# Branch C of the first input gradient chunks by three products, in a convolution stem with group norm and gelu, forward and backward

## The chip, the cores and the metric

The kernel runs on one core of a Trainium2 chip. The metric is device time in microseconds (us) of one execution; lower is better. The engines are TensorE (PE, with weight loads as PEld), VectorE (DVE), ScalarE (ACT), GpSimd (POOL) and the transfer queue that SyncE (SP) issues. Each engine works through its own instructions in a fixed order and waits on semaphores of the others.

## The reference

A strided convolution (stride 2, 31 taps, 256 channels in and out), a normalization over time for each batch and channel, and gelu. All of it is computed together with the gradients for a given `grad_out`:

```python
B, T, D, K = 2, 16000, 256, 31
s = 2
L = (T - K) // s + 1                       # 7985
h = sum(einsum('blc,cd->bld', x[:, i:i + s * L:s, :], w[i]) for i in range(K))
mu = einsum('bld->bd', h)[:, None, :] / L
var = einsum('bld->bd', (h - mu) ** 2)[:, None, :] / L
h = (h - mu) / sqrt(var + 1e-5)
h = h * gn_gamma[None, None, :] + gn_beta[None, None, :]
out = gelu(h)                              # tanh form
out, vjp = jax.vjp(f, x, w, gn_gamma, gn_beta)
grads = vjp(grad_out)                      # of x, w, gn_gamma, gn_beta
```

Inputs and outputs are bf16.

## The kernel before

*Fewer products.* A polynomial product of two halves can be formed with three smaller products instead of four. The kernel nests this over three binary digits of the tap index. The outer two digits are called branch (`br`) and leaf (`lf`); each takes a value of A, B_ or C_, where B_ works on differences or sums of the two halves. So every chunk of time has nine (branch, leaf) products, and a leaf can be cut a third time.

*Three parts.* The forward convolution runs for 2 batches x 4 chunks x 3 branches (stages `F0a` to `F1z`, about 0 to 412 us). The input gradient (`input_grad`, stages `G0a` to `G1z`, about 412 to 822 us) runs over batch `b`, chunk `c`, branch in the order B_, A, C_, and two halves `pr`. The weight gradient (`weight_grad`, stages `Wa` to `Wz`) is the rest. The gelu of batch 0 runs beside the forward pass of batch 1, the gelu of batch 1 (`gelu_batch(1, ...)`, eight units) beside the first input gradient chunks: its gradients are needed when the gradient of batch 1 begins.

*One unit of the input gradient.* There are two forms. `plain` uses the three-way cut for leaf B_ alone (4 matmuls in `g_three_b`, 8 in `g_three_ac`), copies the negated sum to a second accumulator, and then adds leaf A and leaf C_ with 16 matmuls each (`g_leaf`): 44 matmuls. `split` cuts all three leaves: 12 matmuls each, 36 in all. For this, leaves A and C_ need differences of weights (`W2D`, made by `w2_sub`) and the sums that `outer()` makes, and a join (`VP`) of leaf B_ with branch B_'s result. The set `GV` names the chunks that take `split`: in the kernel before, all from chunk (0, 3) on.

*From accumulator to output.* There are four accumulator slots of two banks (`ring`). In each unit ScalarE writes a negated half or whole accumulator (lines 1396 and 868 to `ps`), and `keep` (line 868) copies an accumulator to SBUF as bf16. In `plain`, branches A and C_ are joined with branch B_ by a VectorE instruction that reads the accumulator (`g_join`, line 1411, rate 1); in `split`, a keep writes the output tile `HO` first, and the join reads SBUF. Two tiles `HO` take turns, and `g_store` writes each to memory.

*Around it.* `e_load`, `e_comp` and `e_spread` prepare the next chunk's gradient of `h`: the tiles `EG` and `ET`. `e_spread` copies the two-column overlap of neighbouring chunks (`cp`, line 1296, four GpSimd copies a chunk) and spreads the rest with ScalarE copies (line 1305). A gelu unit loads a half tile of `h`, makes `y` and its square on ScalarE (line 1155), their product with one fused VectorE instruction (line 1157), two sigmoids (lines 1159 and 1161), several VectorE products (line 1167) and sums (line 1180 on ScalarE, 1183 on VectorE). SBUF is one `arena`, divided by hand by byte offsets: tiles overlay each other over time.

*What sets the order.* `Plan.add` records each operation with the tiles it reads and writes. `Plan.order` gives every operation a due time from its successors and a lead from the table `lead`, keyed by stage, helper and caller, lists them on modelled engines, and `emit` issues them in the order of these starts. So the numbers of the table move instructions on all engines. `plan.hold` keeps an operation behind a given matmul; `XPAT` says at which unit of the forward pass each of the eight blocks of x sums (`x_pre`) may be issued.

Of the kernel before, what the change touches and what calls it, by code (L numbers as in the profile page):

```python
# [30 lines left out]
def act(n, extra=0.0):  # L31
    return 0.06 + n * 0.00097 + extra
# [6 lines left out]
class Plan:  # L39
# [3 lines left out]
    def __init__(self, tc):  # L43
# [11 lines left out]
            "F0 conv_stem_kernel wrapper": 109.4,  # L55
            "F0 f_evac last": -1.7,
            "F0 f_join f_evac": 2.6,
            "F0 f_join split": 3.7,
            "F0 f_mm f_three_ac": -0.5,
            "F0 f_mm f_three_b": 0.7,  # L60
            "F0 f_three_b split": -75.0,
            "F0 keep f_evac": 5.3,
            "F0 keep split": -9.5,
            "F0 load conv_stem_kernel": 43.4,
            "F0 load f_evac": 2.8,
            "F0 load put": 0.4,
            "F0 load x_pre": 4.0,
            "F0 load_gb conv_stem_kernel": -22.9,
            "F0 tt f_sums": -3.6,
            "F0 tt second": 5.1,  # L70
            "F0 tt third": -3.4,
            "F0 turn w2_part": 1.2,
            "F0 turn x_load": -6.2,
            "F0 w_sub w2_part": -1.6,
            "F0 x_pre conv_stem_kernel": -0.1,
            "F0 zero conv_stem_kernel": 30.6,
            "F0 zero f_evac": -6.0,
            "F0 zero w2_part": -47.0,
            "F0 zero x_load": -17.6,
            "F0a f_evac last": 8.9,  # L80
            "F0a f_join f_evac": -2.0,
            "F0a f_join split": -16.3,
            "F0a f_mm f_leaf": -12.0,
            "F0a f_mm f_three_b": -24.3,
            "F0a f_mm pe_turn": 7.0,
            "F0a f_three_b f_first": 6.4,
            "F0a f_three_b split": -2.1,
            "F0a keep f_first": -23.9,
            "F0a keep split": -2.3,
            "F0a load load_w": 15.6,  # L90
            "F0a load x_load": 13.2,
            "F0a put x_first": -3.4,
            "F0a tt f_sums": -2.8,
            "F0a tt second": -0.3,
            "F0a tt third": -2.7,
            "F0a turn x_load": -35.7,
            "F0a ve f_first": -3.4,
            "F0a w_sub f_first": -2.1,
            "F0a zero load_w": -15.4,
            "F1 f_evac last": 3.7,  # L100
            "F1 f_join f_evac": 10.3,
            "F1 f_mm f_leaf": 0.3,
            "F1 f_mm f_three_ac": -0.5,
# [1832 lines left out]
```

## Time and profile before

| | us |
|---|---|
| median of three timed runs | 1120.94 (1117.76 to 1122.73) |
| profiled execution, its own time | 1115.62 |
| its span | 1113.8 |
| PE, VectorE, ScalarE, GpSimd busy in the span | 1080.7, 997.6, 605.8, 37.4 |
| first real matmul | 17.86 |
| first matmul of the input gradient | 412.74 |
| mean bandwidth of the transfers | 235 GB/s |

The profile is one execution. Busy times are unions: the records of neighbouring instructions overlap a little. A matmul's record is longer than its share of PE's time, since matmuls overlap too; what one costs is read from how many fit into a full stretch. In the rows of instruction groups, the number behind the bar is the busy time, then follow the mean duration of one in ns and, behind the second bar, the idle time ahead of them and what ended it. In rows of waits the numbers are total, times and longest. In rows in order of time, the first two numbers are start and duration, and a bracket holds the wait ahead.

### The profile page before, as it was taken

The page shows a single profiled execution, that of the slowest core. Times are in us where ns is not written, and L with a number is a line of the kernel's source. Part 1 is how long each engine was busy: PE and PEld are TensorE (multiplying, and loading weights), DVE is VectorE, ACT ScalarE, POOL GpSimd, SP SyncE. Part 2 cuts the span into 40 slices and gives each one's busy share as a digit, 9 for nine tenths or more (in the row PEclk, how much of TensorE's full clock was granted, in tenths as well). Part 3 has the DMA queues.
Part 4 walks back from the last instruction along what each step waited for, and adds up shares of the span by engine and source line. Part 5 has one row for each costly group of instructions (what it writes and reads, how often), then busy time and mean ns, then how long its engine had stood idle before and what let it go on. Part 6 is the DMA issues. An engine that isn't in the chain of part 4 may idle for free. (4 is left out here: it accounts for less than half of the span.)

```text
span 1113.8 us, 19741 instructions
## 1 busy us (share of the span) xinstructions
PE 1080.7 (97%) x8094; PEld 795.8 (71%) x8132; DVE 997.6 (90%) x1039; ACT 605.8 (54%) x838; POOL 37.4 (3%) x67
## 2 busy tenths in 40 slices
PE   5999999999999999999999998999999999999998
PEld 4888899888888984444444443444468888888887
DVE  6995968789999996999899988889789999999996
ACT  1244444688788649797767566676643323332232
POOL 0000000000000010020200011000000000000000
PEclk9999999999999999999999999999999999999999
DMA  9369999995979699987675999988797655696974
GB/s 227 54 178 242 278 268 270 256 175 147 193 169 244 211 288 311 263 231 237 179 244 149 318 317 290 292 286 284 253 297 228 229 205 165 242 326 206 301 213 124
DMA packets 346894, 261.47 MB, mean 235 GB/s; under 512 B 187702, under 2 KB 315572, under 8 KB 340916
## 3 DMA queue, kind: packets, MB, share of 16 engines
q1 hardware_dynamic: 346612, 260.22, 82.4%
q8 instruction: 63, 1.03, 0.4%
q14 instruction: 27, 0.22, 0.1%
q0 software_dynamic: 192, 0.00, 0.0%
HBM read 120.00 MB, written 94.86 MB: 193 GB/s over the span
## 5 line engine op out<-in xcount | busy, mean ns | idle before, releaser
L814 PE MATMUL ps<-arena 128*128 128x256 bf16 (+3 forms) x3668 | 396.7, 271 | 17.0 <-DMA arena<-in_x_dram 7.7
L1369 PE MATMUL ps<-arena 128*128 128x512 bf16 (+1 forms) x1834 | 400.6, 377 | 8.9 <-ACT arena L868 4.2
L814 PEld LDWEIGHTS <-arena 128*128 128x128 bf16 x3668 | 359.0, 99 | 54.4 <-DMA arena<-in_x_dram 8.2
L1369 PEld LDWEIGHTS <-arena 128*128 128x128 bf16 x1872 | 183.6, 98 | 225.2 <-issue 11.7
L868 ACT ACTIVATE arena<-ps 128x1024 bf16<-128x1024 f32 (+1 forms) x187 | 190.0, 1022 | 240.5 <-PE ps L1659 118.5
L1659 PE MATMUL ps<-arena 128*128 128x256 bf16 x2592 | 284.0, 273 | 3.0 <-DVE arena L1613 2.3
L1659 PEld LDWEIGHTS <-arena 128*128 128x128 bf16 x2592 | 253.2, 98 | 34.0 <-DVE arena L1613 3.6
L782 DVE TENSOR_TENSOR arena<-arena 128x2064 bf16<-128x2064 bf16 (+5 forms) x132 | 164.1, 1266 | 26.6 <-PE ps L814 22.8
L1167 DVE TENSOR_TENSOR arena<-arena 128x2048 bf16<-128x2048 bf16 (+1 forms) x80 | 95.4, 1194 | 9.4 <-ACT arena L1159 4.4
L1332 DVE TENSOR_TENSOR arena<-arena 128x1032 bf16<-128x1032 bf16 (+7 forms) x111 | 86.0, 796 | 5.3 <-PE ps L1369 4.8
L1396 ACT ACTIVATE ps<-ps 128x512 f32<-128x512 f32 x108 | 62.8, 586 | 25.3 <-PE ps L1369 25.1
L1155 ACT ACTIVATE arena<-arena,stats 128x1024 bf16<-128x1024 bf16 (+1 forms) x64 | 74.5, 1207 | 1.3 <-DVE stats L1101 0.8
L1555 DVE TENSOR_TENSOR arena<-arena 128x1536 bf16<-128x1536 bf16 (+3 forms) x56 | 62.3, 1124 | 13.3 <-DMA d2d<-arena 12.2
L1622 DVE TENSOR_TENSOR arena<-arena 128x4096 bf16<-128x4096 bf16 x32 | 72.2, 2285 | 0.4 <-DMA arena<-in_x_dram 0.3
L844 ACT ACTIVATE ps<-ps 128x512 f32<-128x512 f32 x59 | 34.3, 582 | 70.2 <-PE ps L814 70.1
L1411 DVE TENSOR_TENSOR arena<-arena 128x1024 bf16<-128x1024 bf16 (+1 forms) x70 | 63.3, 914 | 9.4 <-ACT arena L868 9.0
L1731 ACT COPY ps<-ps 128x512 f32<-128x512 f32 x54 | 30.8, 571 | 64.7 <-PE ps L1659 64.7
L1718 DVE TENSOR_TENSOR arena<-arena 128x2048 bf16<-128x2048 bf16 x54 | 64.7, 1218 | 0.3 <-DMA arena<-d2d 0.3
L1613 DVE TENSOR_TENSOR arena<-arena 128x4096 bf16<-128x4096 bf16 (+1 forms) x32 | 62.1, 1952 | 0.1
L1665 DVE TENSOR_TENSOR arena<-arena 128x1024 bf16<-128x1024 bf16 x75 | 48.8, 684 | 7.8 <-ACT arena L868 7.7
L890 ACT ACTIVATE arena<-ps 128x512 bf16<-128x512 f32 (+1 forms) x64 | 36.7, 579 | 34.8 <-PE ps L814 34.5
L767 DVE TENSOR_TENSOR arena<-arena 128x2048 bf16<-128x2048 bf16 (+1 forms) x45 | 50.5, 1147 | 1.4 <-DMA vl<-arena 1.4
(72 smaller groups left out, 536.9 us busy)
## 6 DMA issues: line engine op xcount, KB each, us to landing
arena<-in_x_dram SPq DMA_DIRECT2D x28, 1024.0 KB, 9.6
arena<-d2d SPq DMA_DIRECT2D x16, 1216.0 KB, 7.4
out_dram<-arena SPq DMA_DIRECT2D x35, 512.0 KB, 4.1
d2d<-arena SPq DMA_DIRECT2D x30, 384.0 KB, 5.6
arena<-dnd SPq DMA_DIRECT2D x10, 960.0 KB, 6.2
arena<-vl SPq DMA_DIRECT2D x9, 1024.0 KB, 8.7
hd<-arena SPq DMA_DIRECT2D x8, 1024.0 KB, 6.8
arena<-in_x_dram SPq DMA_DIRECT2D x32, 256.0 KB, 4.9
```

The costliest lines, as they stand in the source:

```text
L782: lambda: nc.vector.tensor_tensor(out=o, in0=a, in1=b, op=ALU.add))
L814: yield nc.tensor.matmul(ps[:, dh, cs], lhsT=wt, rhs=mv, start=s0, stop=False, skip_group_check=True)
L868: lambda: nc.scalar.activation(out=out, in_=ps, func=ACT.Copy, scale=scale))
L1155: lambda o=o, func=func, i=h[:, dh], sc=sc, bi=bi: SC.activation(out=o, in_=i, func=func, bias=bi, scale=sc))
L1167: add("DVE", dve(8 * wd), [o], [a, b_], lambda: V.tensor_tensor(out=o, in0=a, in1=b_, op=op))
L1332: lambda: nc.vector.tensor_tensor(out=o, in0=a, in1=b, op=ALU.add))
L1369: yield nc.tensor.matmul(ps[:, e, 0:wide], lhsT=lt, rhs=mv, start=s0, stop=False, skip_group_check=True)
L1396: lambda: nc.scalar.activation(out=ps[:, 1], in_=ps[:, 0], func=ACT.Copy, scale=-1.0))
L1411: add("DVE", dve(o.free_size(), rate), [o], [a, b], lambda: nc.vector.tensor_tensor(out=o, in0=a, in1=b, op=op))
L1622: add("DVE", dve(4096), [o], [a, b], lambda: nc.vector.tensor_tensor(out=o, in0=a, in1=b, op=ALU.add))
L1659: yield nc.tensor.matmul(ps[:, s, c0:c1], lhsT=lt, rhs=mv, start=s0, stop=False, skip_group_check=True)
L1718: add("DVE", dve(2048), [d4], [d], lambda: nc.vector.tensor_tensor(out=d4, in0=fan(d[:, o0:o0 + 3 * s + 1:s, :], 1, (o1 - o0) * D), in1=fa ...
```

## The change

Seven edits stand in one diff.

1. `GV` now names branches, and branch C_ of chunks (0, 0), (0, 1) and (0, 2) takes the form `split`. Its two weight differences are made before the first chunk (`w2_outer(True)`), the other four at the old place. `W2D` is laid out anew, so that branch C_'s differences lie at 94208.
2. The gelu tiles `h` of batch 1, which lay there, move to `GREG + 12544` (139968 and 144064), over buffers of the forward pass (`U`, `RB`).
3. In `plain`, branches A and C_ are now kept in `HO` by ScalarE and joined in SBUF. After edit 1 this form is left to branch A.
4. The overlap copies of `e_spread` go from four on GpSimd to two on ScalarE, and its memsets and those of `e_comp` at chunk ends to VectorE.
5. The fused VectorE instruction of gelu (line 1157) becomes an addition of a constant and a product.
6. `leaf_d` of the weight gradient takes both batches in one instruction.
7. `XPAT` issues the eight blocks of x sums at other units, the first at (0, 0, A), and the whole table `lead` has other numbers.

```diff
-            "F0 conv_stem_kernel wrapper": 109.4,
-            "F0 f_evac last": -1.7,
+            "F0 conv_stem_kernel wrapper": 139.4,
+            "F0 f_evac last": -6.4,
...
-    W2D = {(MIR[br], lf): sb(o + 4096 * i, 2, 2, 512) for lf, o in ((B_, 73728), (C_, 94208), (A, 106496)) for i, br in enumerate(ORDER)}
+    W2D = {(MIR[br], B_): sb(73728 + 4096 * i, 2, 2, 512) for i, br in enumerate(ORDER)}
+    W2D.update({(MIR[br], lf): sb(94208 + 8192 * i + 4096 * j, 2, 2, 512) for i, br in enumerate((C_, B_, A))
+                for j, lf in enumerate((A, C_))})
...
-        add("DVE", dve(8 * wd, 1), [z], [y2, y],
-            lambda: V.scalar_tensor_tensor(out=z, in0=y2, scalar=1.0 / GELU_A, in1=y, op0=ALU.add, op1=ALU.mult))
+        add("DVE", dve(8 * wd, 4), [z], [y2],
+            lambda: V.tensor_scalar(out=z, in0=y2, scalar1=1.0 / GELU_A, scalar2=None, op0=ALU.add))
+        add("DVE", dve(8 * wd), [z], [z, y], lambda: V.tensor_tensor(out=z, in0=z, in1=y, op=ALU.mult))
...
-            zero(EG[:, :, 0, 0, 231:HM], 50)
-            zero(EG[:, :, 0, 1:4, 230:HM], 156)
-            zero(EG[:, 0, 1, :, 230:HM], 104)
-            zero(EG[:, 1, 1, :, 230:HM], 104)
+            v = EG.rearrange("p d e k f -> p d (e k) f")
+            zero(v[:, :, 0, 231:HM], 50, "DVE")
+            zero(v[:, :, 1:8, 230:HM], 364, "DVE")
...
-            def cp(o, i):
-                add("POOL", 0.3, [o], [i], lambda: nc.gpsimd.tensor_copy(out=o, in_=i))
-            for dh in range(2):
-                cp(et[:, dh, 0:3, :, 0:2], et[:, dh, 0:3, :, 256:258])
-            cp(et[:, :, 3, 0, 0:2], et[:, :, 3, 0, 256:258])
-            cp(et[:, :, 3, 1, 0:1], et[:, :, 3, 1, 256:257])
+            for o, i in ((ev[:, :, 0:7, 0:2], ev[:, :, 0:7, 256:258]), (ev[:, :, 7, 0:1], ev[:, :, 7, 256:257])):
+                add("ACT", act(o.free_size()), [o], [i], lambda o=o, i=i: nc.scalar.copy(out=o, in_=i))
...
-    GV = {(b, c) for b in range(NB) for c in range(NCK) if (b, c) >= (0, 3)}
+    EARLY = (C_,)
+    GV = {(b, c, br) for b in range(NB) for c in range(NCK) for br in ORDER if (b, c) >= (0, 3) or (br in EARLY and c in (0, 1, 2))}
...
+                elif True:
+                    keep(ho[:, :, j, :], ps[:])
+                    g_join(ho[:, :, j, :], ho[:, :, j, :], rb, ALU.subtract if (br == A) == (lf == A) else ALU.add, 2)
...
-                        (split if (b, c) in GV else plain)(b, c, pr, br, P * pr, sums)
+                        (split if (b, c, br) in GV else plain)(b, c, pr, br, P * pr, sums)
...
-                for b in range(NB):
-                    o_ = 2 if i3 == A else 0
-                    add("DVE", dve(2304), [DL[i3, b]], [D2[b]], lambda b=b, i3=i3, o_=o_: nc.vector.tensor_tensor(
-                        out=DL[i3, b], in0=D2[b][:, o_:o_ + 17:2, :], in1=D2[b][:, 1:18:2, :], op=ALU.subtract))
+                o_ = 2 if i3 == A else 0
+                w_two("leaf_d", [DL[i3, b] for b in range(NB)], [t[:, o_:o_ + 17:2, :] for t in D2], [t[:, 1:18:2, :] for t in D2], ALU.subtract, D2)
...
-          {"h": (94208, 98304), "y": (102400, 106496), "s": (110592, 114688), "y2": (GREG,), "z": (GREG + 4096,), "o": (), "g": (GREG + 8192,)})
-    XPAT = {u: i for i, u in enumerate([(0, c, br) for c in range(1, 4) for br in ORDER][:4 * len(PRE)])}
+          {"h": (GREG + 12544, GREG + 16640), "y": (102400, 106496), "s": (110592, 114688), "y2": (GREG,), "z": (GREG + 4096,), "o": (), "g": (GREG + 8192,)})
+    XPAT = {(0, 0, A): (0,), (0, 1, B_): (1, 2), (0, 1, C_): (3,), (0, 2, A): (4,), (0, 2, C_): (5,), (0, 3, B_): (6, 7)}
...
+    w2_outer(True)
     ge = gelu_batch(1, GT[1], *PACE[1])
...
-            w2_outer()
+            w2_outer(False)
```

Two places show what this does to the order. The first is ScalarE in chunk (0, 0), where branch C_ begins. Line 1396 (1403 after the change) is a half negation, line 868 (880) to `ps` a whole negation and to `arena` a keep, line 1305 (1312) a spread copy, 1155 (1167) gelu's `y` and square, 1159 and 1161 (1172 and 1174) its sigmoids, 1180 (1193) its sums. Before:

```order
L1396 ACTIVATE ps0_114<-ps0_114 128x512
L1305 COPY arena_110<-arena_110 128x3x256 x4
L1305 COPY arena_110<-arena_110 128x2x256
L868 ACTIVATE ps1_115<-ps0_114 128x1024
L1305 COPY arena_110<-arena_110 128x2x256
L1159 ACTIVATE arena_110<-arena_110 128x2048
L1161 ACTIVATE arena_110<-arena_110 128x2048
L1396 ACTIVATE ps2_116<-ps2_116 128x512
L1155 ACTIVATE arena_110<-arena_110,stats_101 128x1024 x2
L868 ACTIVATE ps3_117<-ps2_116 128x1024
L1180 ACTIVATE arena_110,esum1_108<-arena_110 128x1024
```

After, at the same place of the chunk:

```order
L1172 ACTIVATE arena_110<-arena_110 128x2048
L880 ACTIVATE arena_110<-ps3_117 128x2x512
L880 ACTIVATE arena_110<-ps0_114 128x1024
L1403 ACTIVATE ps2_116<-ps2_116 128x512
L1174 ACTIVATE arena_110<-arena_110 128x2048
L1403 ACTIVATE ps0_114<-ps0_114 128x512
L880 ACTIVATE arena_110<-ps1_115 128x2x512
L1403 ACTIVATE ps3_117<-ps3_117 128x512
L880 ACTIVATE arena_110<-ps2_116 128x2x512
L1312 COPY arena_110<-arena_110 128x3x256
L1403 ACTIVATE ps1_115<-ps1_115 128x512
L1312 COPY arena_110<-arena_110 128x2x256
```

Between two sigmoids of one gelu unit now stand two keeps and a half negation, and keeps of 2 x 512 to the output tile stand among the spread copies, where before two whole negations and gelu's own instructions stood.

The second place is the transfer queue of SP where the forward pass ends: `hd1_0` is `h` of batch 1, chunk 0 (half tiles of 2 x 1024 for gelu), `vl1`, `vl2` and `vl0` are the input gradient's weights of branches B_, C_ and A, the two transposes from `arena` turn the first chunk's gradient, and `dnd0` takes it. Before:

```order
L609 DMA arena_110<-hd1_0_64 128x2x1024
L609 DMA arena_110<-dyd0_0_68 128x4096
L609 DMA arena_110<-hd1_0_64 128x2x1024
L609 DMA arena_110<-vl1_58 128x4x1024 x3
L609 DMA arena_110<-vl2_59 128x4x1024 x3
L614 DMA_TRANSPOSE arena_110<-arena_110 128x16x128 x2
L614 DMA_TRANSPOSE arena_110<-in_grad_out_dram 128x8x256
L609 DMA hd1_3_67<-arena_110 128x4096
```

After:

```order
L619 DMA arena_110<-vl1_58 128x4x1024 x2
L619 DMA arena_110<-vl2_59 128x4x1024 x3
L624 DMA_TRANSPOSE arena_110<-arena_110 128x16x128 x2
L619 DMA arena_110<-hd1_0_64 128x2x1024
L619 DMA arena_110<-vl0_57 128x4x1024
L624 DMA_TRANSPOSE arena_110<-in_grad_out_dram 128x8x256
L619 DMA hd1_3_67<-arena_110 128x4096
```

The first half tile of `h` for gelu moved from ahead of the weights to behind the two transposes; the second half follows seven rows later.

More of the change, by code (lines that the diff above doesn't have):

```diff
@@ L63, in __init__ @@
[L63 to L74, printed above, removed]
-            "F0 x_pre conv_stem_kernel": -0.1,
@@ L89, in __init__ @@
[L89 to L102, printed above, removed]
@@ L157, in __init__ @@
[L157 to L169 removed]
+            "F1 tt f_sums": -8.6,
@@ L203, in __init__ @@
+            "G1 keep split": -1.0,
             "G1 load d2_piece": 0.8,
@@ L262, in __init__ @@
[L262 to L272 removed]
+            "G1 tt first": 3.7,
+            "G1 tt outer": 6.0,
```

389 lines of the change are left out of this document (211 added, 178 removed).

## The prediction

> **What bounds the kernel now.** I read the page's busy times, then the waits of PE (the TensorE matmuls), then stretches of the span, then ScalarE's own waits in the stretch that the change rewrites.
>
> ```profile
> PE 1080.7 (97%) x8094; PEld 795.8 (71%) x8132; DVE 997.6 (90%) x1039; ACT 605.8 (54%) x838; POOL 37.4 (3%) x67
> ```
> ```profile
> PE ps L814 <- DMA arena<-in_x_dram: 7.7, 3, 4.5
> PE ps L814 <- DVE arena L767: 5.8, 1, 5.8
> PE ps L1369 <- ACT arena L868: 4.2, 3, 2.7
> PE ps L1659 <- DVE arena L1613: 2.3, 2, 1.2
> ```
> ```profile
> 422.40:586.00 163.60, 160.19 (x742) 73.88 (x755) 150.84 (x171) 129.90 (x144) 14.90 (x16) 1.00 0.80 240
> 586.00:632.00 46.00, 45.74 (x212) 21.07 (x216) 46.00 (x59) 31.27 (x45) 0.23 (x4) 1.00 0.76 241
> ```
>
> PE is idle for 33.1 us of the 1113.8 us span, and 13.5 us of that are the two opening waits. So PE bounds the kernel nearly everywhere, and a matmul removed is time saved, as long as the engines beside it keep up. The columns of the stretches are length, PE, weight loads, VectorE (DVE), ScalarE (ACT), GpSimd (POOL). From 422.4 to 586 us (chunks 0 to 2 of the first input gradient, with the second gelu batch beside them) PE idles 3.4 us, VectorE 12.8, ScalarE 33.7. The row behind it shows VectorE at 46.0 of 46.0 us while PE lost 0.26: a saturated neighbour need not stop PE if the order suits.
>
> **The change, part by part.** *Matmuls.* Branch C of three chunks, two halves each, goes from 44 matmuls (4 + 8 + 16 + 16) to 36 (three times 4 + 8): 6 x 8 = 48 fewer, all 512 wide.
>
> ```profile
> 588.00:616.00 28.00, 27.89 (x131) 12.78 (x131) 28.00 (x38) 18.84 (x27) 0.23 (x4) 1.00 0.62 166
> ```
> 27.89 / 131 = 0.213 us each, so PE's work falls by 10.2 us, to 150.0 us in that stretch.
>
> *ScalarE.* The durations, each the mean of one:
>
> ```profile
> L868 ACT ACTIVATE arena<-ps 128x1024 bf16<-128x1024 f32 x186 | 188.9, 1022 | 235.7 <-PE ps L1659 118.5 <-PE ps L1369 52.3 <-PE ps L814 36.4
> L1396 ACT ACTIVATE ps<-ps 128x512 f32<-128x512 f32 x108 | 62.8, 586 | 25.3 <-PE ps L1369 25.1
> L868 ACT ACTIVATE ps<-ps 128x1024 f32<-128x1024 f32 x24 | 24.1, 1006 | 7.5 <-PE ps L1369 4.1 <-PE ps L814 3.3
> L895 ACT ACTIVATE arena<-ps 128x2 bf16<-128x2 f32 x2 | 0.4, 178 | 0.0
> ```
> Between the square root that opens the second batch's gelu and that batch's last sum, the order of before has 12 keeps, 18 half negations and 16 full negations on ScalarE; the order of after has 41, 30 and 10, and four overlap copies (0.18 us each, by the small activation L895). That adds 29 x 1.022 + 12 x 0.586 - 6 x 1.006 + 4 x 0.18 = 31.4 us. Rows of neighbours overlap: the 146 rows of before there sum to 142.0 us where the stretch shows 129.9, 0.083 us a row, so 39 more rows give back 3.2. ScalarE then needs 129.9 + 28.2 = 158 us where PE needs 150. From here ScalarE is the bound: the stretch cannot fall below 158 us, and of the 10.2 us at most 163.6 - 158 = 5.6 reach the end. To this come ScalarE's own waits on others.
>
> ```profile
> ACT arena L1180 <- DVE arena L1167: 8.0, 4, 3.6
> ACT arena L1159 <- DVE arena L1157: 7.5, 4, 2.4
> ACT arena L1305 <- POOL arena L1296: 3.8, 1, 3.8
> ```
> These are its waits in this same stretch. The third goes with the GpSimd copies. The first two, 15.5 us, are gelu's ping-pong with VectorE. Where another keep is ready, the order can put it into the gap, as the excerpts of chunk 0 show; between none (158) and all of it left (173.5) I take 5.5 us, nearer the full end of the row at 586 us, where a saturated engine lost almost nothing: 163.5, so 0 us gained in this stretch, bounds -5.6 to +10.
>
> *VectorE there.* The rows for the joins, the sums and the gelu pieces:
>
> ```profile
> L1411 DVE TENSOR_TENSOR arena<-arena 128x2048 bf16<-128x2048 bf16 x30 | 36.6, 1218 | 7.5 <-ACT arena L868 7.5
> L1332 DVE TENSOR_TENSOR arena<-arena 128x2064 bf16<-128x2064 bf16 x12 | 14.8, 1230 | 0.2
> L1411 DVE TENSOR_TENSOR arena<-ps,arena 128x1024 bf16<-128x1024 f32 x24 | 29.2, 1217 | 2.0 <-ACT arena L1155 2.0
> L1411 DVE TENSOR_TENSOR arena<-arena 128x1024 bf16<-128x1024 bf16 x40 | 26.8, 686 | 1.9 <-ACT arena L868 1.5
> L1157 DVE SCALAR_TENSOR_TENSOR arena<-arena 128x2048 bf16<-128x2048 bf16 x12 | 27.4, 2286 | 6.3 <-ACT arena L1155 6.2
> L1163 DVE TENSOR_SCALAR arena<-arena 128x2048 bf16<-128x2048 bf16 x12 | 8.2, 684 | 0.0
> L1167 DVE TENSOR_TENSOR arena<-arena 128x2048 bf16<-128x2048 bf16 x60 | 73.0, 1219 | 4.8 <-ACT arena L1159 2.8 <-ACT arena L1161 1.6
> ```
> The joins of branches A and C read SBUF: 24 x (1.217 - 0.686) = 12.7 us less. Six joins of 2048 (1.218) and three sums of 2064 (1.230) are new: 11.0 us. Eight gelu fusions become two instructions each: 8 x (2.286 - 0.684 - 1.219) = 3.1 us less. The two early weight differences leave a later place, the few memsets taken from GpSimd are near 0.1 us each. In sum 150.8 - 12.7 + 11.0 - 3.1 = 146.0 us.
>
> A join in SBUF thus costs 1.022 + 0.686 us over two engines where it cost 1.217 on one: a gain where VectorE is the bound, a loss where ScalarE is. For branch C it comes with the shorter form; for branch A's 12 joins it is a choice. The Trainium skill ("VectorE: DVE Perf Modes", section Rules for kernel authors) speaks against the choice: read a matmul's output directly at the slow rate, or copy it to SBUF first if many operations follow; here one follows. By that rule branch A would leave ScalarE 158 - 12 x (1.022 - 0.083) = 146.7 us and VectorE 146.0 + 12 x 0.531 = 152.4, so the stretch would end at 152.4 where the change makes it 158, and the change as made would give 5.6 us away.
>
> *Moved gelu tiles.* The first unit's half h tile overlays buffers that the last forward matmuls read, so its load can be issued only after them and behind two transposes on SP, where before it stood ahead of the weight loads.
>
> ```profile
> 413.60 0.75 PE L814 MATMUL ps<-arena 128*128 128x230 bf16 x6
> 423.56 4.63 ACT L1155 ACTIVATE arena<-arena,stats 128x1024 bf16<-128x1024 bf16 x4 [0.82 <-DVE stats L1101]
> arena<-hd SPq DMA_DIRECT2D x16, 512.0 KB, 4.6
> ```
> Forward matmuls end at 414.4 us; with the median 4.6 us to landing the tile is there at 419, before the 423.6 at which the statistics let gelu start. Cost 0; twice the landing time would add 0.1 us, so the bound is +2. Behind the late tile would wait gelu's squares and all keeps after them.
>
> *GpSimd copies to ScalarE.* The second place is where chunk (1, 0) begins:
>
> ```profile
> 671.48 1.02 ACT L868 ACTIVATE arena<-ps 128x1024 bf16<-128x1024 f32 x1 [5.25 <-DMA out_dram<-arena]
> 672.55 10.31 PE L1369 MATMUL ps<-arena 128*128 128x512 bf16 x39 [2.68 <-ACT arena L868]
> 677.20 4.13 POOL L1296 COPY arena<-arena 128x12 bf16<-128x12 bf16 x4 [32.42 <-DVE arena L1332]
> 683.99 16.35 PE L1369 MATMUL ps<-arena 128*128 128x512 bf16 x74 [1.12 <-ACT arena L868]
> 672.00:700.00 28.00, 26.21 (x113) 11.51 (x115) 24.16 (x34) 19.49 (x27) 4.13 (x4) 0.94 1.02 299
> ```
> Four copies took 4.13 us and PE then waited 1.12; two short ScalarE copies take that away: -1.1 (0 to -1.1). The 2.68 us before it come from a keep that waits for a store of the output tile, and cost more than they last: the next 39 matmuls took 10.31 us where 39 x 0.213 = 8.3, and the granted clock of this stretch is 0.94 (1.00 in the stretches above). That store is ordered among the same transfers after the change; I keep it, with -4.7 (2.68 + 2.0) as the far end.
>
> *The rest.* PE's waits beside the first gelu batch, and the rows of the weight gradient and of the start:
>
> ```profile
> 233.70 36.54 PE L814 MATMUL ps<-arena 128*128 128x256 bf16 x332 [1.02 <-ACT ps L868]
> 276.61 28.21 PE L814 MATMUL ps<-arena 128*128 128x256 bf16 x256 [0.67 <-ACT ps L844]
> 305.78 14.40 PE L814 MATMUL ps<-arena 128*128 128x256 bf16 x130 [0.95 <-ACT arena L890]
> L1777 DVE TENSOR_TENSOR arena<-arena 128x2304 bf16<-128x2304 bf16 x36 | 47.9, 1351 | 2.4 <-DMA arena<-d2d 2.4
> L1622 DVE TENSOR_TENSOR arena<-arena 128x4096 bf16<-128x4096 bf16 x32 | 72.2, 2285 | 0.4 <-DMA arena<-in_x_dram 0.3
> L782 DVE TENSOR_TENSOR arena<-arena 128x2064 bf16<-128x2064 bf16 x41 | 50.3, 1233 | 19.9 <-PE ps L814 18.9 <-DMA arena<-in_x_dram 0.9
> 4.74 1.88 SPq L609 DMA_DIRECT2D arena<-in_x_dram  x1
> ```
> The eight gelu units beside the forward pass save another 3 us of VectorE; PE idled 1.02 + 0.67 + 0.95 = 2.6 us there: -1 (0 to -2.6). In the weight gradient 36 differences of 1.351 us become 18; a row of 4096 takes 2.285, so one of 4608 takes about 2.55 and 18 x 0.15 = 2.7 us of VectorE go, against PE's 2.3 us of waits on that engine: -1 (0 to -2.3).
>
> At the start the three x loads go ahead of the weights on SP. The last of them was issued at 4.74 us before, behind four weight loads, and can now go some 2 us sooner. On VectorE two more sums (1.233 us each) stand ahead of the first weight difference, while one difference of 1.219 us drops behind the one that the first real matmul needs: 2.5 - 1.2 - 2 = -0.7, say -0.5 (-2 to +1.5). One block of x sums moves into the first chunk's transfers, where PE waits for transfers only at its opening (the 7.7 us, three times): 0, at worst +1.
>
> **Sum.** 0 - 1.1 - 1 - 1 - 0.5 = -3.6, say -4 us. The profiled execution's own time is 1115.6 us; the three timed runs have a median of 1120.9 (1117.8 to 1122.7), so it lies below all of them. I carry the difference over to the median: 1117 us. About 0.5%, 5.6 us, is what a measurement of this kernel can tell from no change.
>
> **Rivals.** *ScalarE runs without gaps* (0.27): the stretch takes its 158 us (-5.6), and chunk (1, 0) loses the longer stall too (-4.7): -3.6 - 5.6 - 4.7 = -13.9, 1107 us. For it: VectorE's 46.0 of 46.0 us without hurting PE. Against it: three engines at 146, 150 and 158 us of work in one stretch, each in fixed order.
>
> *ScalarE's waits stay* (0.23): gelu's second half waits for VectorE as before, and behind each wait stand keeps that free PE's accumulators; 15.5 us on 158 is 173.5, +10, less 3.6: +6 to +7, 1127 us, slower. It decides from about 9 us of ScalarE waiting in the stretch. For it: the 15.5 us, and PE's waits are on ScalarE there already. Each gap in PE like that at 672.55 would add 2 us more. The Trainium skill ("TensorE: Matmul & The Clock Gate", section What's actually happening) says that an idle window of about 3.4 us halves the clock; here 2.68 us of idling already went with slower matmuls.
>
> *The output tiles block* (0.12): the 24 new keeps write the two output tiles and wait, on ScalarE, for the store two units earlier; VectorE's joins waited there before. One store as late as at 671.48 costs PE 2.7 + 2.0 us: about +1, 1122 us. Against it, a store of this size lands in 4.1 us and a unit lasts 36 or 44 x 0.213 = 7.7 or 9.4:
>
> ```profile
> out_dram<-arena SPq DMA_DIRECT2D x35, 512.0 KB, 4.1
> ```
>
> **Chances.** The forecast has 0.38. Its own spread (-8 to -1) puts 0.14 of it beyond -0.5%. Faster: 0.14 + 0.27 = 0.41. Slower: 0.20 of the second rival and 0.02 of the third: 0.22. Same: 0.37. The range from 1105 to 1129 leaves out the ends of both outer rivals.
>
> **What would show it.** Right: 8046 PE rows, ScalarE near 636 us, VectorE near 988; from the first square root after the forward pass to chunk 3 ScalarE busy over 95% and PE's waits there on ScalarE, over 8 us in all; no GpSimd copies. Wrong: PE above 98% busy in that stretch (first rival), ScalarE waiting over 9 us there for VectorE's gelu products (second), for stores (third), or PE's waits moved to the forward or the weight gradient, which I took as settled though every row there is reordered.

## The result, and the profile after

The changed kernel takes 1113.9 us (median of nine runs, 1113.2 to 1117.2) against 1120.9 us on the same chip (nine runs, 1115.3 to 1124.7): ratio 0.995, 95% interval 0.9929 to 0.997. The forecast was 1117, between 1105 and 1129. The new profiled execution took 1116.1 us and that of before 1115.6, so the two profiles differ by nothing while the runs differ by 7 us. That was the question to settle.

The busy times of the page and the stretches after: from the first real matmul to the second square root, from there to the last ScalarE sum, to the first matmul of the weight gradient, and to the end (columns as in the prediction).

```profile
PE 1074.8 (96%) x8046; PEld 792.6 (71%) x8084; DVE 989.9 (89%) x1054; ACT 634.5 (57%) x886; POOL 10.5 (1%) x27
```
```profile
17.50:417.80 400.30, 399.34 (x3661) 359.24 (x3664) 350.10 (x394) 233.53 (x382) 5.45 (x10) 1.00 0.88 213
417.80:583.30 165.50, 154.96 (x699) 70.49 (x712) 150.76 (x195) 156.95 (x184) 1.54 (x4) 0.98 0.82 243
583.30:819.70 236.40, 230.34 (x1050) 105.01 (x1070) 202.84 (x241) 155.38 (x212) 1.18 (x3) 0.99 0.91 282
819.70:1114.30 294.60, 285.82 (x2592) 253.95 (x2592) 276.55 (x210) 85.19 (x108) 0.53 (x1) 0.99 0.71 220
```

The counts are as forecast: 8046 matmuls, ScalarE 634.5 us, VectorE 989.9. In the second stretch ScalarE is busy for 157.0 of 165.5 us, which is 94.8% (the prediction's sign was over 95%). It is now the busiest engine there, and PE idles 10.5. The same stretch of before, and the rest of it:

```profile
422.40:586.40 164.00, 160.53 (x743) 74.04 (x757) 151.24 (x171) 130.30 (x146) 14.90 (x16) 1.00 0.80 239
586.40:822.70 236.30, 231.04 (x1055) 105.43 (x1075) 206.64 (x242) 152.84 (x204) 10.18 (x23) 0.99 0.90 278
822.70:1113.80 291.10, 283.98 (x2593) 253.21 (x2592) 277.63 (x228) 85.61 (x108) 0.53 (x1) 1.00 0.72 226
```

PE's busy time in the second stretch is 5.6 us less, not the 10.2 of the 48 matmuls: the others ran slower, at a granted clock of 0.98 where it was 1.00 before. The stretch is 1.5 us longer. PE's waits there, after:

```profile
PE ps L1376 <- ACT ps L1403: 5.2, 4, 2.9
PE ps L1376 <- ACT ps L880: 2.9, 1, 2.9
PE ps L1376 <- DVE arena L1339: 1.4, 1, 1.4
PE ps L1376 <- ACT arena L880: 0.2, 1, 0.2
```

Two waits of 2.9 us make up more than half. The first, on PE, and what stands on ScalarE ahead of the half negation (line 1403) that ends it:

```profile
465.81 1.90 PE L1376 MATMUL ps<-arena 128*128 128x512 bf16 x8 [1.37 <-DVE arena L1339]
470.60 45.02 PE L1376 MATMUL ps<-arena 128*128 128x512 bf16 x199 [2.89 <-ACT ps L1403]
```
```profile
465.44 4.63 ACT L1167 ACTIVATE arena<-arena,stats 128x1024 bf16<-128x1024 bf16 x4
469.96 0.58 ACT L1403 ACTIVATE ps<-ps 128x512 f32<-128x512 f32 x1
```

The matmuls that the negation needs ended at 467.7 us; four gelu activations stood before it until 470.0. ScalarE did not stop. It did the wrong work first. Its waits for VectorE's gelu products, 15.5 us before, are 2.6 us in this stretch:

```profile
ACT arena L1193 <- DVE arena L1180: 1.3, 2, 0.8
ACT arena L1172 <- DVE arena L1170: 1.3, 3, 0.7
```

### The profile page after: what moved, and what is told of

Read it like the earlier page. It is cut to its first block, busy times and chain, and to the rows that moved or that the text cites. A ratio compares the mean times of both kernels' runs of the same rounds, so it can differ in the third digit from the quotient of the medians.

```text
span 1114.3 us, 19639 instructions
## 1 busy us (share of the span) xinstructions
PE 1074.8 (96%) x8046; PEld 792.6 (71%) x8084; DVE 989.9 (89%) x1054; ACT 634.5 (57%) x886; POOL 10.5 (1%) x27
## 5 line engine op out<-in xcount | busy, mean ns | idle before, releaser
L1376 PE MATMUL ps<-arena 128*128 128x512 bf16 (+1 forms) x1786 | 394.6, 380 | 16.1 <-ACT ps L1403 5.2
L880 ACT ACTIVATE arena<-ps 128x1024 bf16<-128x1024 f32 (+1 forms) x217 | 219.7, 1021 | 228.2 <-PE ps L1671 136.8
L794 DVE TENSOR_TENSOR arena<-arena 128x2080 bf16<-128x2080 bf16 (+7 forms) x132 | 164.7, 1268 | 32.6 <-PE ps L826 31.2
L1625 DVE TENSOR_TENSOR arena<-arena 128x4096 bf16<-128x4096 bf16 (+2 forms) x50 | 107.3, 2168 | 2.8 <-PE ps L1671 2.8
L1339 DVE TENSOR_TENSOR arena<-arena 128x1032 bf16<-128x1032 bf16 (+7 forms) x114 | 90.2, 809 | 13.9 <-PE ps L1376 12.8
L1418 DVE TENSOR_TENSOR arena<-arena 128x1024 bf16<-128x1024 bf16 (+1 forms) x100 | 87.0, 877 | 13.0 <-ACT arena L880 12.7
L1403 ACT ACTIVATE ps<-ps 128x512 f32<-128x512 f32 x120 | 69.9, 587 | 28.1 <-PE ps L1376 27.5
L856 ACT ACTIVATE ps<-ps 128x512 f32<-128x512 f32 x59 | 34.3, 582 | 77.6 <-PE ps L826 77.2
```

Of the source, the lines that this page charges most:

```text
L794: lambda: nc.vector.tensor_tensor(out=o, in0=a, in1=b, op=ALU.add))
L880: lambda: nc.scalar.activation(out=out, in_=ps, func=ACT.Copy, scale=scale))
L1339: lambda: nc.vector.tensor_tensor(out=o, in0=a, in1=b, op=ALU.add))
L1376: yield nc.tensor.matmul(ps[:, e, 0:wide], lhsT=lt, rhs=mv, start=s0, stop=False, skip_group_check=True)
L1418: add("DVE", dve(o.free_size(), rate), [o], [a, b], lambda: nc.vector.tensor_tensor(out=o, in0=a, in1=b, op=op))
L1625: add("DVE", dve(o.free_size()), outs, ins, lambda: nc.vector.tensor_tensor(out=o, in0=a, in1=b, op=op), kind=kind + " weight_grad")
```

## The experiments

*The changed kernel once more.*

> The changed kernel once more, as the control on this chip and as a second sample of its profile. Expected: a ratio to before of 0.993 to 0.997, and in the profile again the stretch from the second batch's square root to its last ScalarE sum at about 165 us with ScalarE busy for 157 of them. Where PE's small waits fall should differ from the first profile, the sum of them by a few us.

1114.1 us (1110.4 to 1116.1, nine runs), ratio 0.9942 (0.9923 to 0.9961). Its profile shows the same stretches (205.1, 165.5, 236.6 and 294.4 us from the first square root on) and the same two waits of 2.9 us. So the comparison of profiles is no accident of one of them on this side.

*What binds the second stretch: less ScalarE.*

```diff
-  lambda o=o, a0=a0, sv=sv: SC.activation(out=o, in_=sv, func=ACT.Copy, accum_out=a0))
+  lambda o=o, a0=a0, sv=sv: SC.activation(out=o if b == 0 else o[:, :, 0:8], in_=sv if b == 0 else sv[:, :, 0:8], func=ACT.Copy, accum_out=a0))
```

> The changed kernel in the same order on every engine; only ScalarE's 16 sums over the second batch's gelu gradient (line 1193) run over 32 elements instead of 1024 or 928, so the gradients of gamma, beta and x of that batch are not computed rightly. This takes about 16 x 0.82 = 13 us from ScalarE in the first three chunks of the input gradient and nothing from any other engine. Theory (ScalarE is the bound there): ScalarE needs 144 us, less than PE's 150, so the stretch falls from 165 to 155 to 158 us and the kernel by 7 to 10 us. Rival (VectorE, or the order in which the three engines hand over, holds the stretch): the stretch stays within 2 us of 165, ScalarE is idle for the difference, and the kernel gains under 2 us.

*Less VectorE.* The same with the 16 product sums of VectorE (`tensor_tensor_reduce`) cut to 8 columns:

> The counterpart on VectorE: the changed kernel in the same order, only VectorE's 16 product sums of the second batch's gelu (line 1196 or near it, 1.2 us each) run over 32 elements, so the same gradients are wrong. This takes about 16 x 1.0 = 16 us from VectorE in the same stretch. Theory (ScalarE is the bound): the stretch loses 0 to 2 us. Rival (VectorE is): it loses 7 us or more.

The first gave 1109.6 us (ratio 0.9911, 0.9886 to 0.9935), the second 1113.2 (0.9945, 0.9929 to 0.9961). The second stretch, of the one and of the other:

```profile
417.30:578.60 161.30, 151.38 (x697) 69.29 (x709) 149.97 (x194) 145.69 (x184) 1.54 (x4) 1.00 0.85 250
```
```profile
418.40:584.70 166.30, 155.60 (x699) 70.62 (x711) 137.43 (x199) 157.20 (x184) 1.54 (x4) 0.97 0.82 242
```

13.3 us off VectorE shorten nothing: VectorE does not bind. 11.3 us off ScalarE shorten the stretch by 4.2 and the kernel by 4.5, which is neither expectation. ScalarE's total binds only in part, since PE's longest wait (2.9 us, the one above) stays even then. PE's idle time in the stretch goes from 10.5 to 9.9 us and no further; the other 3.6 us are PE's busy time (155.0 to 151.4), at a granted clock of 1.00 where the changed kernel's profile has 0.98.

*What the 48 matmuls are worth: put them back, order unchanged.*

```diff
-            g_three_b(ring[x], br, B_, pl[B_], o)
+            g_three_b(ring[x], br, B_, pl[B_], o, br == C_ and (b, c) < (0, 3))
...
-            g_three_b(ring[k], br, C_, pl[C_], o)
+            g_three_b(ring[k], br, C_, pl[C_], o, br == C_ and (b, c) < (0, 3))
```

> The changed kernel with 48 matmuls more: in branch C of chunks 0 to 2 two of the three first-tap products of each half issue their four matmuls twice (the repeat starts the sum afresh, so nothing else changes), with the order on every other engine word for word that of the changed kernel. 48 x 0.213 = 10.2 us of PE are put back, ScalarE and VectorE stay. Theory (ScalarE is the bound from the square root to the last ScalarE sum, 157 of 165.5 us): PE's idle time there (10.5 us) takes up most of the added work, the stretch grows by 2 to 5 us, and the kernel by as much, to 1116 to 1119. Rival (PE is still the bound and its waits stand beside its work): the stretch grows by 9 to 11 us and the kernel goes to about 1124, above the kernel before; then the 48 matmuls were worth their full 10.2 us and ScalarE's keeps cost about as much again.

1120.7 us (1116.3 to 1124.0), ratio 1.0012 (0.9989 to 1.0035).

```profile
418.30:588.30 170.00, 161.82 (x760) 74.05 (x758) 152.61 (x197) 157.57 (x185) 1.61 (x4) 1.00 0.80 237
```

The stretch grew by 4.5 us and the median by 6.5, against 10.2 us of work. Again in between: of each microsecond put back on PE 0.4 (stretch) to 0.6 (median) arrives, and of each taken from ScalarE 0.4.

*The two longest waits: a matter of order.*

```diff
-        return sorted(range(n), key=lambda i: (self.start[i], i))
+        return ahead(self, sorted(range(n), key=lambda i: (self.start[i], i)))
...
+def ahead(plan, rows):
+    ops, start = plan.ops, plan.start
+    acts = [i for i in rows if ops[i]["eng"] == "ACT"]
+    place = {i: (start[i], 0, i) for i in rows}
+    for i, most in {1585: 2, 1692: 3}.items():
...
+        while j > k - most and ops[acts[j - 1]]["kind"].endswith("gelu_batch") and start[acts[j - 1]] > ready - 0.2:
+            j -= 1
...
```

> The changed kernel with two negations moved forward in ScalarE's queue, nothing else: the half negation that stood behind four gelu activations stands behind two, and the whole negation that stood behind two ScalarE sums and two gelu activations stands behind one sum. ScalarE has the same 157 us of work in the stretch. Theory (the two longest waits of PE there, 2.9 us each, come from the places of these two negations in the queue): about 2 us of each wait goes, and with it some of the slower matmuls behind them; stretch 161 to 163, kernel 1110 to 1112. Rival (ScalarE without gaps is the bound and order does not matter): the waits come back at the next negations, within 1 us of the changed kernel.

1112.5 us (1110.1 to 1113.9), ratio 0.9931 (0.9906 to 0.9955), so 1 to 2 us better than the changed kernel, a difference that the intervals do not separate. The stretch fell to 162.3 us:

```profile
418.50:580.80 162.30, 153.29 (x715) 69.72 (x713) 150.87 (x195) 156.52 (x185) 1.54 (x4) 1.00 0.84 248
```

PE's waits at the two places:

```profile
469.07 1.89 PE L1376 MATMUL ps<-arena 128*128 128x512 bf16 x8 [0.62 <-ACT ps L1403]
472.27 17.43 PE L1376 MATMUL ps<-arena 128*128 128x512 bf16 x80 [1.31 <-ACT ps L880]
536.31 4.48 PE L1376 MATMUL ps<-arena 128*128 128x512 bf16 x20 [1.61 <-ACT arena L880]
```

Where PE waited 2.89 us it now waits 0.62 and, one step on, 1.31; where it waited 2.91, 1.61. Of the 3.2 us by which the stretch got shorter, about half is PE's idle time (10.5 to 9.0 us) and half its busy time (155.0 to 153.3, at a clock of 1.00). That supports the theory, though 162.3 is still 6 us above ScalarE's work.

*Branch A's joins from the accumulator (edit 3 undone).*

```diff
-                elif True:
+                elif False:
```

> The changed kernel with one edit undone: branch A of the first three chunks is joined by VectorE straight from the accumulator again, without the 12 keeps. ScalarE loses 12 x 0.94 = 11 us in the stretch, VectorE gains 12 x 0.53 = 6 us: 146 and 157 us of work. By the rule to read a matmul's output directly when one operation follows, the stretch should fall from 165 to 158 to 161 us and the kernel by 4 to 7 us. Rival: the table of leads was made for the other form, VectorE at 157 us becomes the next bound, and its joins free the accumulators later; then the kernel stays within 2 us or is up to 5 us slower.

1129.9 us, ratio 1.0092 (1.0058 to 1.0127): 16 us slower than the changed kernel, but this edit lists the whole program anew. Its stretches from the first square root on:

```profile
214.00:419.90 205.90, 204.09 (x1859) 181.77 (x1859) 188.07 (x229) 154.81 (x228) 3.53 (x7) 1.00 0.83 205
419.90:588.10 168.20, 159.81 (x730) 73.28 (x744) 157.31 (x196) 149.62 (x175) 1.54 (x4) 0.98 0.79 238
588.10:822.10 234.00, 223.91 (x1020) 101.87 (x1039) 203.12 (x242) 151.75 (x209) 1.18 (x3) 0.99 0.90 278
822.10:1124.80 302.70, 286.07 (x2592) 253.90 (x2592) 275.49 (x209) 84.81 (x107) 0.53 (x1) 0.98 0.70 220
```

From the square root to the weight gradient it takes 168.2 + 234.0 = 402.2 us, where the changed kernel takes 165.5 + 236.4 = 401.9. In the input gradient, then, the two kernels come out alike; the first of its two stretches holds one wait of PE of 6.47 us, at 471.64 us, for a spread copy of ScalarE, which the new order may have brought too. The loss that this profile shows stands in the weight gradient (8 us, with one wait of 7.8 us for a transfer) and ahead of the second square root (2 to 3), where branch A's joins play no part. So the order that was listed anew cost it, and the run does not settle what edit 3 alone is worth.

*Where the forward pass got shorter.* Between the square roots before takes 208.1 us and the changed kernel 205.2. Two parts of the change were put into the kernel before, the numbers of the forward pass alone (with the way `XPAT` splits the x sums), and gelu's two operations alone, at the old place. The edit of the second:

```diff
-        add("DVE", dve(8 * wd, 1), [z], [y2, y],
-            lambda: V.scalar_tensor_tensor(out=z, in0=y2, scalar=1.0 / GELU_A, in1=y, op0=ALU.add, op1=ALU.mult))
+        def two():
+            yield V.tensor_scalar(out=z, in0=y2, scalar1=1.0 / GELU_A, scalar2=None, op0=ALU.add)
+            yield V.tensor_tensor(out=z, in0=z, in1=y, op=ALU.mult)
+        add("DVE", dve(8 * wd, 1), [z], [y2, y], two)
```

> The kernel before with the order numbers of the forward pass, and the way the x sums of a chunk are split, taken from the changed kernel; gelu's two-step product and all of the input gradient stay as before. Theory (the forward pass is 4.5 us shorter because the numbers list its rows better): the square root comes at 417 to 419 us and not 422.4, the kernel ends at 1115 to 1118. Rival (the 3 us of VectorE that the two-step product saves beside the first batch's gelu make it shorter): the square root stays within 1.5 us of 422.4 and PE's waits on ScalarE at the gelu units (1.02, 0.67, 0.95) stay.

> The kernel before with gelu's one fused VectorE operation (2.286 us) issued as the two operations of the changed kernel (0.684 and 1.219 us), at the same place in the order; every other row on every engine stays as it was. Theory (part of the forward pass's shorter time comes from VectorE's lighter gelu): from the first to the second square root 8 x 0.38 = 3.1 us of VectorE go, and PE's waits on ScalarE beside the first gelu batch (1.02, 0.67, 0.95) shrink: 206 to 207 us between the square roots where before had 208.1 to 208.5, the kernel 1 to 2 us faster. Rival (the order made it): 208 us between the square roots, the kernel within 1 us of before. Third possibility, since the order was listed for the long operation: a little slower.

The numbers alone gave 1135.2 us (1.0129, 1.0091 to 1.0168) and 213.5 us between the square roots: far worse. The two operations alone gave 1119.7 us (1.0002, 0.9977 to 1.0027), 208.9 us, and PE's waits about as before:

```profile
234.50 42.24 PE L814 MATMUL ps<-arena 128*128 128x256 bf16 x384 [1.55 <-ACT ps L868]
277.41 28.21 PE L814 MATMUL ps<-arena 128*128 128x256 bf16 x256 [0.67 <-ACT ps L844]
306.57 107.13 PE L814 MATMUL ps<-arena 128*128 128x256 bf16 x1014 [0.95 <-ACT arena L890]
```

Both theories fell. A lighter VectorE by itself does not shorten this stretch, and neither do the numbers by themselves; which edits together made it shorter stays open.

*The weight gradient* takes 294.4 to 294.6 us after, 291.1 to 293.3 before. The merged differences were issued as two again, at the same place. (The expectation counts 16; the profile has 18 rows more on VectorE, so all 18 were split.)

```diff
+            def go():
+                for i in range(2) if kind == "leaf_d" and len(outs) == 2 else ():
+                    yield nc.vector.tensor_tensor(out=outs[i], in0=as_[i], in1=bs[i], op=op)
...
-            add("DVE", dve(o.free_size()), outs, ins, lambda: nc.vector.tensor_tensor(out=o, in0=a, in1=b, op=op),
-                kind=kind + " weight_grad")
+            add("DVE", dve(o.free_size()), outs, ins, go, kind=kind + " weight_grad")
```

> The changed kernel with 16 of the 18 merged differences of the weight gradient (4608 wide, 2.55 us) issued as two of 2304 (1.35 us each), at the same place in the order; every other row stays. VectorE gets 16 x 0.15 = 2.4 us more in the weight gradient. Theory (merging helps, as the prediction had it, and the 2 to 3 us that the weight gradient takes longer come from the order of its rows): it goes from 294.4 to 295 to 297 us. Rival (the long merged rows hold up what PE waits for, above all before the wait of 2.1 us): it falls to 292 to 293.

1115.1 us (0.9963, 0.9939 to 0.9986) and 293.7 us in the weight gradient. That lies between the two expectations: merging brings nothing that can be measured, and the longest wait, 2.07 us on VectorE at the combination that begins at 1013 us, is there in both forms (and in the third profile of the kernel before, at 1019 us). So the order remains the likelier cause of the longer weight gradient; it was not tested by itself.

*The kernel before, profiled again.* None of this explains the 6 to 7 us between the runs.

> The kernel before, unchanged, for a second profile of it. The first profiled execution took 1115.6 us where the runs have a median of 1120.3 to 1120.9. Theory: the executions of this kernel differ by some 4 us, and the profiled one was a fast one; a second profile near the median shows in which stretch the 4 to 5 us stand. Rival: profiled executions are faster than timed ones by themselves; then this one comes out at 1115 to 1116 again while its timed runs keep the median.

> The kernel before, unchanged, for a third profile. Two profiled executions took 1115.2 and 1115.6 us, with medians of the timed runs of 1119 to 1121. Theory (profiled executions of this kernel are fast by themselves): 1115 to 1116 again, with the same stretches (208, 164, 235 to 236, 291 to 292 us from square root to square root, to the last ScalarE sum, to the weight gradient and to the end). Rival (chance): near 1120, and one of these stretches holds the 4 to 5 us.

The second profile was like the first (1115.2 us; runs 1118.9). The third took 1120.8 us, near its runs' median of 1119.7, and showed what the others lacked. Its stretch behind the last ScalarE sum is 2.2 to 3.4 us longer, with 15.3 us of GpSimd where the others have 10.2:

```profile
587.30:825.80 238.50, 231.80 (x1076) 105.50 (x1074) 206.73 (x242) 152.92 (x205) 15.30 (x23) 0.99 0.89 275
```

The overlap copies near 642 us on GpSimd, the spread copy behind them on ScalarE, and PE, in the third profile. (Counted from 412.7 us on, 264 matmuls to a chunk in `plain` and 216 in `split`, chunk (1, 0) runs from about 632 to 682 us. So this place lies in it and not in chunk (0, 3), where the last expectation below puts it, and the place at 672 to 684 us, where the prediction has chunk (1, 0) begin, is its end.)

```profile
641.72 7.99 POOL L1296 COPY arena<-arena 128x12 bf16<-128x12 bf16 x4 [36.75 <-DVE arena L1332]
649.35 0.83 ACT L1305 COPY arena<-arena 128x768 bf16<-128x768 bf16 x1 [7.07 <-POOL arena L1296]
650.72 2.72 PE L1369 MATMUL ps<-arena 128*128 128x512 bf16 x6 [6.05 <-ACT ps L1396]
```

In the first profile these are 2.85 us on GpSimd, a wait of 1.12 on ScalarE, and one of 0.25 on PE. Behind the spread copy, in ScalarE's queue, stood the two half negations that PE needed. The copies by themselves (minimum, median and maximum in ns, with the first and last start), in the third profile and then in the first:

```profile
L1296 POOL COPY arena<-arena x4: 180/187/7601, 641.7 to 649.5; 128x12 bf16<-128x12 bf16 x2, 128x4 bf16<-128x4 bf16 x1, 128x2 bf16<-128x2 bf16 x1
```
```profile
L1296 POOL COPY arena<-arena x4: 503/670/1185, 641.9 to 644.1; 128x12 bf16<-128x12 bf16 x2, 128x4 bf16<-128x4 bf16 x1, 128x2 bf16<-128x2 bf16 x1
```

One copy of 12 elements per partition took 7.6 us; the three behind it 0.19 each. VectorE's rows over the same time, in the third profile, from the one that runs when the copy starts to the last before VectorE stops:

```profile
640.87 1.90 DVE L1332 TENSOR_TENSOR arena<-arena 128x1032 bf16<-128x1032 bf16 x3
...
648.54 0.68 DVE L1332 TENSOR_TENSOR arena<-arena 128x1032 bf16<-128x1032 bf16 x1
649.15 0.18 DVE L1226 TENSOR_TENSOR small<-stats,small 128x2 f32<-128x2 f32 x1
```

VectorE ran operations with two SBUF inputs without a gap until 649.33 us, and the copy ended there. The Trainium skill ("SBUF — State Buffer", section Summary: rules for kernel authors) says that a VectorE operation with two SBUF inputs and a GpSimd operation that reads SBUF exclude each other, the later one waiting until the first has finished. The trace agrees that the copy waits, but here it waited for a whole run of operations, not for one. In the first profile VectorE's row has no gap there either, and the same copy was done after 0.50 us. The run with gelu's two operations shows the stall once more:

```profile
641.12 7.96 POOL L1298 COPY arena<-arena 128x12 bf16<-128x12 bf16 x4 [36.74 <-DVE arena L1334]
650.10 36.40 PE L1371 MATMUL ps<-arena 128*128 128x512 bf16 x160 [5.97 <-ACT ps L1398]
```

So two of the four profiles with these copies at this place (executions of 1115.2 and 1115.6 us) lack the stall, and two (1120.2 and 1120.8 us) have it.

*That one edit by itself.*

```diff
-                add("POOL", 0.3, [o], [i], lambda: nc.gpsimd.tensor_copy(out=o, in_=i))
+                add("POOL", 0.3, [o], [i], lambda: nc.scalar.copy(out=o, in_=i))
```

> The kernel before with its 24 small overlap copies (2 to 12 elements per partition) issued on ScalarE and not on GpSimd, at the same place in the list; every row of PE, VectorE and SP stays, and nothing of the other edits is in. Theory (most of the 5 to 6 us that the changed kernel gains over the runs of before, though no two profiles show it, is the stall behind the GpSimd copies of chunk (0, 3): 7.99 us for four copies and 6.05 us of PE idle time in the profile of 1120.9 us, 2.85 and none in those of 1115): the copies take 0.2 us each, PE's 6.05 us wait near 650 us does not come, the median falls from 1119.5 to 1114.5 to 1116 and the runs lie closer together than 8 us. Rival (the scatter comes from elsewhere, and the gain from the forward pass): the median stays within 1.5 us of before and the scatter too; 20 added ScalarE rows may even cost 1 us.

1112.9 us (six runs, 1111.5 to 1116.0) against 1119.0 (1116.4 to 1122.1): ratio 0.9941 (0.9921 to 0.9962). One line in the kernel before gives what the whole change gives. PE's wait near 650 us is gone:

```profile
642.52 0.29 ACT L1296 COPY arena<-arena 128x12 bf16<-128x12 bf16 x2
```
```profile
425.80:587.50 161.70, 160.97 (x757) 73.98 (x756) 151.37 (x171) 131.07 (x152) 2.15 (x8) 1.00 0.82 242
587.50:821.30 233.80, 230.75 (x1077) 105.19 (x1075) 206.39 (x242) 153.67 (x218) 2.02 (x11) 1.00 0.90 280
```

Both stretches are shorter than in any profile of before (163.9 and 235.1 at best). In the first of them the copies took 5.2 us near 542 us in every profile of before, ScalarE waited 3.8 us for them, and PE 1.30 some 7 us later; that wait of PE is gone too. The six runs lie within 4.6 us, those of before within 5.7 to 9.4. But two kernels without GpSimd copies (the 48 matmuls put back, the differences split) scatter over 7.7 and 9.6 us, so how much of the scatter the copies make is not shown. Against this kernel the changed one saves 3.6 us between the square roots (208.8 to 205.2) and loses 3.8, 2.6 and 2.6 us in the three stretches behind (161.7 to 165.5, 233.8 to 236.4, 292.0 to 294.6). Its other six edits together come to about nothing. That is a difference between two kernels: the changed kernel with its copies back on GpSimd was not run, and the profile of the kernel with the copies moved, at 1115.1 us, is slower than that kernel's median, with its first square root at 217.0 us where those of before have it at 213.5 to 214.8.

The fastest kernels with all of the computation in them are this one and the one with two negations moved; 1112.9 and 1112.5 us can't be told apart. The two edits were not tried together.

## Why the prediction was right, and where it was wrong

The time (1117, range 1105 to 1129; 1113.9 measured) and the direction held. Several steps held as well, but nearly all of the gain came from a term that was priced at 1.1 us, so that the sum came near the measured time partly by luck.

*Matmuls and the new bound.* Right in the numbers. ScalarE needs 157.0 us in the stretch where 158 was worked out, PE waits there for ScalarE 8.3 us (over 8 was named), and the stretch came out at 165.5 us where 163.5 was forecast, inside the bounds. That nothing is left of 10.2 us of matmuls came out as argued, but the mechanism did so only in part. The step took ScalarE's total as a floor with gaps beside it. In the runs, work taken off ScalarE or put back on PE arrives by about half, some of it as a change of the granted clock, and 3.2 us of the stretch hung on the place of two negations. The prediction looked for these waits in gelu's ping-pong with VectorE; those are only 2.6 us after, and what PE waited for stood behind gelu activations in ScalarE's own queue. VectorE came out at 150.8 us where 146.0 was worked out; with 13.3 us less of it the stretch was no shorter, so nothing hung on that.

*Branch A's joins.* By the rule that the prediction cites from the Trainium skill ("VectorE: DVE Perf Modes", section Rules for kernel authors) the change would have given 5.6 us away. In the input gradient the kernel that follows the rule was no faster (402.2 against 401.9 us). The trace does not bear the rule out here, but the order differs too, so that its price stays open.

*Moved gelu tiles.* Right, 0: nothing waits for the late load.

*GpSimd copies.* This step failed. It priced the place where the profile showed PE waiting, 1.12 us at 683.99 us, and called it -1.1. That gain did not come there (PE waits 1.73 and 2.27 us at this place after, 2.68 and 1.12 before). By the run that moves the copies alone the edit is worth 6.1 us. The profiles show where: 2.2 us in the stretch from the square root to the last ScalarE sum, and behind it 1.3 to 2.5 us against the profiles in which the copies near 642 us were short, as in the one that the prediction read (2.85 us), and 4.7 against the one in which they were not (7.99). The warning stood in the rows: copies of the same 12 elements took from 0.19 to 3.96 us. And it stood in the text: the profiled execution "lies below all of" the timed runs, and "I carry the difference over to the median". Part of that difference was this stall: the third profile's span is 5.3 us longer than the first's, with 2.2 us of it in the stretch of the stall and 2.2 in the weight gradient. How many of the timed runs had the stall is not known.

*The longer stall near 672 us.* It was kept, and it stayed, somewhat shorter: 1.73 and 0.91 us in the two profiles of the changed kernel, 2.68 and 2.09 in the first two of before.

*The rest.* -1 was forecast for the forward pass, 3 us came between the square roots, within a little more than the bound of 2.6. The reason given, VectorE's lighter gelu, fell with the run that did only that. -1 was forecast for the weight gradient; it got 1.1 to 3.5 us longer, and the merged differences bring nothing. The warning that every row there is reordered was the right one. For the start -0.5 was forecast; the first real matmul came at 17.47 and 16.74 us in two profiles after, at 17.86 before.

In place of the sum of -4 stands about -6 for the copies and near 0 for all else, in which, against the profile with the copies moved, -3.6 in the forward pass, +9 behind it and a first square root that comes 4.4 us earlier cancel.

## What to carry to other kernels

When a profiled execution is faster than all timed runs, it may lack something that they have: profile again until one falls near the median, and compare the two before any edit is priced. A small copy on GpSimd beside long runs of VectorE took 0.18 to 7.6 us here, so look at the longest row of such an operation and at what stands behind it in the queue of the engine that waits. Where two engines are both near their limit, total work says little; read which instruction PE waits for and what stands ahead of it, for here moving two rows shortened the stretch by 3.2 us, and putting 48 matmuls back lengthened it by 4.5.

## What the runs showed of the hardware

A GpSimd copy of 12 elements per partition lasted 7.6 us, until a gap came in VectorE's row of operations with two SBUF inputs; on ScalarE each of the 24 copies took 0.19 to 0.21 us. In the same kernel and the same place that copy took 0.50 us in another execution, and what decides between the two stays open.

PE's waits can cost more than they last. Behind the two waits of 2.9 us of the changed kernel the granted clock falls, and behind the shorter ones of the kernel with two negations moved it does not; the same two pieces, of the one and of the other:

```profile
465.80:516.00 50.20, 46.82 (x208) 21.30 (x214) 45.85 (x58) 47.22 (x54) 0.00 (x0) 0.97 0.84 242
516.00:540.00 24.00, 19.64 (x81) 8.35 (x81) 22.30 (x30) 22.69 (x28) 0.00 (x0) 0.93 0.73 222
```
```profile
466.50:516.70 50.20, 46.59 (x216) 21.16 (x217) 47.67 (x61) 48.93 (x55) 0.00 (x0) 1.00 0.89 255
516.70:541.00 24.30, 22.06 (x100) 9.78 (x100) 23.29 (x31) 23.70 (x30) 0.00 (x0) 1.00 0.76 213
```

The Trainium skill ("TensorE: Matmul & The Clock Gate", section What's actually happening) puts the idle window that lowers the clock at about 3.4 us; here 2.9 us already went with 0.97 and 0.93, and waits up to 1.6 us with 1.00. But in these traces the length of a wait alone does not decide it. At the first of the two places PE waited 3.44 us in the kernel with the 48 matmuls put back and 3.43 us in the one with the differences split; over the ten microseconds in which that wait ended, the clock was 1.00 in the one and 0.83 in the other:

```profile
470.00:480.00 10.00, 6.56 (x32) 2.86 (x31) 9.86 (x14) 10.00 (x10) 0.00 (x0) 1.00 0.96 304
```
```profile
470.00:480.00 10.00, 7.46 (x27) 3.07 (x27) 9.87 (x14) 8.36 (x8) 0.00 (x0) 0.83 0.96 303
```
